# Complex state pairs in one tile: two-diagonal matrices, a scan over 64 cells and sums by three routes in a gated SSM and linear-attention kernel

## The chip, the cores and the metric

The kernel runs on one core of one Trainium2 chip. The metric is the device time of one execution in microseconds, as a median over runs. TensorE (PE) multiplies matrices into PSUM, VectorE (DVE) and ScalarE (ACT) compute between PSUM and SBUF, GpSimd (POOL) and SyncE (SP) here mostly issue DMAs.

## The reference

The input x has 2048 rows of 512 features. Two branches are mixed row by row with a gate g = sigmoid(x · gate_w):

```
Lam_bar = exp(dt * Lam)                      # 512 complex states
B_bar   = ((Lam_bar - 1) / Lam)[:, None] * B
h_t     = Lam_bar * h_{t-1} + B_bar x_t      # t = 0 .. 2047
a       = 2 * Re(C h_t) + x * Dskip
q, k, v = x @ wqkv                           # 32 heads of 16
pq, pk  = q @ w_phi, k @ w_phi               # per head
phi     = [softmax(p), softmax(-p)]          # 32 features for q and for k
b       = (phi_q (phi_k^T v)) / (phi_q sum(phi_k) + 1e-6) @ wo     # not causal
out     = g * a + (1 - g) * b
```

B, C, Lam and h are complex; re and im come as separate inputs, and all inputs are bf16. The output is bf16.

## The kernel before

**Tiling.** The 2048 rows are taken as 256 cells of 8 consecutive rows; a row's place in its cell is its residue r. `xT` holds x transposed with the rows sorted by residue, so that a strided slice gives all 256 cells of two residues r and r+4: 512 columns. Rows leave in 16 output tiles of 128 (128 cells of one residue), in the order of residues 7, 3, 5, 1, 0, 4, 2, 6. The 512 states are four tiles of 128 (index j), each with a re and an im half of its own.

**An order written by hand.** Every part of the work is a generator whose name is a token (`st_q` is `q0` to `q15`, and so on). The list `ORDER` of 841 tokens runs each generator on to its next `yield`, and no scheduler stands behind it: the list alone sets the order of instructions on every engine, and of the DMA issues on SP and POOL. `@n` after a token names the PSUM banks (eight in all) for the tiles it opens; `:D` puts an eviction or a scaling (`evac` L129, `scaled` L436 on ACT, L438 on DVE) on DVE where it would be on ACT.

```
    for tok in ORDER.split():
        tok, _, banks = tok.partition("@")
        tok, _, eng = tok.partition(":")
        sel["eng"] = "dve" if eng == "D" else "act"
        sel["banks"] = [int(b) for b in banks]
        next(st[tok])
```

**The attention branch.** `W`, `T`, `f`, `w` prepare weights and the first two tiles of x; x comes through SP in transposes (`Lx`), B in `Lb`, Q's weight in `Lq`, C in `Lc`. `k`, `v`, `q` (L483) make keys, values and queries for 128 rows by four matmuls each of 480 or 512 columns with an eviction (`Xq`, `vx`; `vx` is one of eight buffers). The features are two softmaxes over 16 values per head, for four tiles at a time: maximum tree `x`/`X` (L531), minimum `n`/`N`, subtractions into `EE` (L542, L548), exponential `e`/`E` (L554), sum tree and logarithm `s`/`S` (L562), division (L569 for keys; for queries only the ratio of the two sums is multiplied in, L581). For queries, `S` ends with two DMA transposes on SP into `phT` (`phT0` for the first four tiles, then two buffers in turn). `a` (L599) multiplies keys' features with values into two PSUM banks over all 16 tiles; in its loop L603 adds the gate's x · gate_w with matmuls of one column, 64 in all. `Y` masks the result into `KVm`. `o` (L835) multiplies `phT` with `KVm`, takes the logarithm of the denominator (L839), its negative exponential with the gate (L842), and scales into `on` (L848).

**The state branch.** With λ = Lam_bar, `M` and `M2` compute powers of λ in small tables, `D` makes nine sets of diagonal matrices `dg` (re, im and minus im of λ, λ², λ⁴) for the four j. `b` (L613) multiplies `BT` with two residues of x, `g` (L625) with the residues 1 and 5, 3 and 7, and adds in PSUM what the diagonals make of earlier rows of the cell: four real products for each complex one, over the two tiles re and im. In `g`'s second half, V (four rows summed, evicted by L129 into `vv`) is multiplied by λ⁴ (256 columns) and added, so that `vv` holds the sum over a cell. `i` makes rotation tables `T2c` and `T2s` for 256 cells, `z` turns the complex recurrence into real ones: two multiplications and two additions, a scan along 256 cells for re and one for im (L678), two multiplications (L681, L684) and two additions back, for each j. This gives the state at each cell's last row, in `H3`. `H` (`st_h4`) gives the state at row 3 of each cell from it (λ⁴ by two scalings and three additions on DVE). `h` then adds λ² times these to the local sums in `H1` (residues 1 and 5), and `p` adds λ times to those in `eb` (residues 0, 4 and 2, 6): each by row scalings on ACT or DVE, followed for j = 2 and 3 by three DVE operations, and for j = 0 and 1 by adding DMAs on POOL's queue (L648), which add one SBUF tile into another. `c` scales C by B_bar's factor into `C2`, again with an adding DMA for each j.

**The end.** `y` (L816) multiplies the states with `C2` for an output tile, eight matmuls of 512 columns; the skip term x · Dskip is added by four matmuls of 128 columns with a diagonal `Dd` (L823), or, for the tiles in the list `XD`, on DVE (`u`, L854). `O` transposes `on` to `oT` by DMA on SP (L862), `t` multiplies it with `Wo` into the same PSUM bank (L875) and evicts with the gate (L879 on DVE, L881 on ACT), `R` (L891) sends pairs of tiles out. `Z` (L316) is a matmul on a zero tile while the first inputs are under way. `G` (L748 and its neighbours) makes the sigmoid from the 16 gate columns.

Of the kernel before, what the change touches and what calls it, by code (L numbers as in the profile page):

```python
# [10 lines left out]
ALU = mybir.AluOpType  # L11
# [9 lines left out]
P = 128  # L21
# [15 lines left out]
N0 e4 z1 z1 H1 s2 g200 g200 g201 H1 g210@6 g211@3 g210 s4 H1 c1 g211 g210 q7@4 v4 s4 h0 h0 H1 H1 g210 h0 a2 a2 a2 a2
h1 h1 s4 s3 q4 s3 s4 g211 g211 q5@2 q5 q6@0 g211 X0 N0 q7 q6 g211 g210 X1 b300@7 g210 z2 b300 z2 p00:D z2 z2 z2 b311@4
p00 z2 b301@0 E0 X1 z2 b301 z2 E0 X1 v13@7 g301@6 s4 q9@0 b310@3 z2 b311 s4 z2 g301 g300@2 H2 S0 X1 S0 g301 g300 H2:D
S0 h1 b310 g310@4 g300 N1 S0 p10 c3 S0 h1:D h1 N1 s4 g311@6 q9 g311 g311 g311 g310 g310 g310 S0 S0 s4 p10 p10 H2 q10@2  # L40
g311 S0 g311 g310 g310 z3 z3 v13 H2 p00 H2 z3 z3 z3 v8@0 v8 v10@3 h0 z3 v10 p10 N1 v12@4 v12 z3 z3 S0 S0 h0 q8@0 p10
q8 z3 z3 v9@7 v9 v14@3 h2 h2:D H3:D H3:D p00:D v14 v15@0 v15 h2 v11@4 H3 a3 N1 a3 v11 a3 a3 a4 H3 q11@4 H3 a4 a4 h2 h2
a4 X1 N1 Y Y p11 h3 p11 y1@0 G y1 h3 y1 h3 Y Y q11 q10 X2 N2 G h3 h3 END q12@2 o1@4 o0@6 E1 X2 E1 o0 q14@1 q14 N2 o1
y6@3 y6 X2 N2 X2 S1 o0 o0 S1 q12 o1 y6 S0 p01 o1 q15@1 S1 N2 q15 q13@2 q13 p11 o3@6 y0@1 o3 S1 S1 p00 y0 X2 p30 o2@4
S1 o2 S1 o2 y0 N2 S1 o2 N3 o3 G Ld Ld E2 E2 y7@2 y7 S1 y7 y3@4 y3 y3 N3 p20 p01 X3 G o3 S2 O0 t0 t0 t1 t1 y5@5 S1 S1
X3 o4@6 O1 S2 o4 o4 N3 R0 o5@0 S2 S2 o5 o5 o4 o5 O2 S2 S2 N3 X3 X3 p30 y5 y5 y4@6 y4 S2 S2 o6@0 p01 p11 p01 o6 o6 X3
y2@7 p20 N3 E3 E3 p20 o6 p20 p20 t3 y2 y2 t2 t5 y4 t2 t3:D t4 t4 S2 S2 y10@4 o9@0 o9 o8@6 p30 p30:D p30 p11 y10 u9 S3
t5 o8 o8 o9 o8 o9 y11@5 o7@6 p01 y11 y9@0 S2 p21 S3 o7 S3 S3 O4 o7 o7 p31 p21:D y9 S3 S3 y8@1 S3 o10@6 R1 u8 o10 o10
S3 S3 y8 o10 p31 t8 o11@6 O3 t9 S3 S3 t6 o11 o11 p21 p31 t8 t9 y12@1 t7 p31:D y14@0 t6 t7 o11 o12@6 o12 p21 O5 p21
o13@2 u11 p31 y14 o12 o12 o13 y12 o13 R2 o14@6 o13 O6 o14 o14 o14 R4 u10 O7 y13@2 y13 o15@6 o15 o15 o15 t10 t10 R3 t11  # L50
t13 t11 u12 O8 u13 t12 t12 t13 u14 R5 t14 t14 R6 y15@54 y15 y15 t15 t15:D t15 R7 t15 R8 R8
# [4 lines left out]
XD = (8, 9, 10, 11, 12, 13, 14)  # L56
KO = tuple(range(16))
XLOADS = ((2, 2), (4, 2), (6, 2), (8, 2), (10, 2), (12, 2), (14, 2))
# [12 lines left out]
def kernel(  # L71
# [24 lines left out]
    PT = Pst // P  # L96
    NTI = S // P
# [42 lines left out]
    vec_n = const.tile([12, P], BF16, name="vec_n")  # L140
# [5 lines left out]
    C2 = const.tile([P, 2, PT, D], BF16, name="C2")  # L146
    warm = const.tile([P, D], BF16, name="warm")
    nc.vector.memset(warm[:], 0.0)
    nc.scalar.dma_start(out=Wc[:], in_=B_w_phi.rearrange("(k hl) e f -> (hl e) k f", hl=8))
    wk_nat, xn = C2[:, 0], C2[:, 1]  # L150
# [4 lines left out]
    for n, src in enumerate((A_Lambda_im, A_Lambda_re, A_log_dt)):  # L155
        nc.gpsimd.dma_start(out=vec_n[4 * n:4 * n + 4, :], in_=src.rearrange("(j p) -> j p", p=P))
# [6 lines left out]
    vec = const.tile([P, 5, KT], F32, name="vec")  # L163
# [791 lines left out]
```

## Time and profile before

| | |
|---|---|
| median of three runs | 151.08 us (150.99 to 151.36) |
| span of the profiled execution | 149.4 us |
| outside the span, against the median | 1.7 us |
| TensorE busy, matmuls | 142.8 us (96%), 1010 |
| VectorE busy, instructions | 139.0 us (93%), 338 |
| ScalarE busy, instructions | 125.1 us (84%), 222 |
| GpSimd busy, instructions | 26.6 us (18%), 42 |
| moved by DMA | 20.14 MB, mean 135 GB/s |

The span is the profiled execution's own time, from its first to its last instruction; the median is that of separate runs, which hold what lies before and after it. Times in the profile count from the span's start. An instruction's busy time runs from its start to its end, and neighbours on one engine may overlap a little, so the sum of the busy times is over the time that the engine needs in a full queue. In the rows, an operation is written as line, engine, operation, output<-input and shape (partitions x elements); "idle before" is the time that the engine stood before it, with what ended most of it.

### The profile page before, as it was taken

What the parts mean: (1) busy time and instruction counts of PE and PEld (TensorE: products, weight loads), DVE (VectorE), ACT (ScalarE), POOL (GpSimd) and SP (SyncE); (2) the same over time, 40 slices, a digit from 0 to 9 for tenths busy, and PEclk for the clock granted to TensorE, in tenths of its full rate; (3) what the DMA queues carried; (4) which work ended last, traced back from release to release, by engine and by line L of the source; (5) the groups of instructions that cost most, each with busy time, mean ns of one, the idle gap of its engine ahead of it and who ended that gap; (6) DMA issues with size and microseconds to landing.
All of it is one profiled execution on the core that took longest, in us unless ns stands there. A gap on an engine that the chain in (4) does not pass through costs nothing.

```text
span 149.4 us, 2839 instructions
## 1 busy us (share of the span) xinstructions
PE 142.8 (96%) x1010; PEld 73.8 (49%) x1010; DVE 139.0 (93%) x338; ACT 125.1 (84%) x222; POOL 26.6 (18%) x42
## 2 busy tenths in 40 slices
PE   6999999999999999999999999999999999999980
PEld 2844444545545444464444467555444554455450
DVE  2899999999999999999999999999999999986880
ACT  3479999999999999999999999999989996552000
POOL 7403700000000341022605236011004200000000
PEclk9999999999999999999999999999999999999999
DMA  4999999991220174008274999908999996998742
GB/s 118 222 235 174 142 202 176 246 189 33 54 91 0 26 114 77 0 0 140 38 107 70 166 175 183 210 7 133 103 238 218 184 186 77 227 207 197 209 148 71
DMA packets 52959, 20.14 MB, mean 135 GB/s; under 512 B 44496, under 2 KB 52432, under 8 KB 52944
## 3 DMA queue, kind: packets, MB, share of 16 engines
q1 hardware_dynamic: 48000, 15.44, 53.1%
q0 software_dynamic: 4000, 4.20, 18.6%
q10 hardware_dynamic: 944, 0.31, 0.8%
q8 instruction: 8, 0.13, 0.4%
q14 instruction: 7, 0.06, 0.1%
HBM read 2.91 MB, written 2.10 MB: 33 GB/s over the span
## 4 chain that ended last, share of the span: by engine, by line
ACT 67%; PE 24%; issue 3%; DVE 2%
ACT EE L554 15%; PE PS L816 11%; ACT Xq L129 9%; PE PS L875 7%; ACT CT L436 6%; ACT vx L129 5%; ACT dg L436 4%; ACT H L129 3%; ACT vv L129 3%; ACT eb L129 3%; ACT Bn L129 3%; PE PS L316 2%; PE PS L835 2%; ACT lg L562 2%; ACT m L436 1%
## 5 line engine op out<-in xcount | busy, mean ns | idle before, releaser
L554 ACT ACTIVATE EE<-EE 128x2048 bf16<-128x2048 bf16 x16 | 32.5, 2066 | 0.2 <-DVE EE L548 0.2
L483 PE MATMUL PS<-WKV,xT 128*128 128x480 bf16 (+1 forms) x128 | 29.3, 373 | 0.2 <-DMA xT<-in_A_x_dram 0.2
L483 PEld LDWEIGHTS <-xT 128*128 128x128 bf16 x192 | 18.1, 98 | 19.4 <-DMA xT<-in_A_x_dram 0.7
L129 ACT CAST Xq<-PS 128x480 bf16<-128x480 f32 x32 | 20.1, 735 | 0.5 <-PE PS L483 0.5
L625 PE MATMUL PS<-xT,BT 128*128 128x512 bf16 x64 | 15.9, 379 | 0.0
L816 PE MATMUL PS<-C,H 128*128 128x512 bf16 x64 | 15.4, 378 | 0.5 <-DVE on L848 0.2
L875 PE MATMUL PS<-Wo,oT 128*128 128x512 bf16 (+2 forms) x68 | 15.5, 367 | 0.0
L613 PE MATMUL PS<-xT,BT 128*128 128x512 bf16 x64 | 15.4, 379 | 0.0
L483 PE MATMUL PS<-Wq,xT 128*128 128x480 bf16 x64 | 15.1, 366 | 0.0
L848 DVE TENSOR_TENSOR on<-PS,rd 128x512 bf16<-128x512 f32 x16 | 10.7, 681 | 2.3 <-ACT rd L842 2.3
L881 ACT ACTIVATE ot<-PS,G 128x512 bf16<-128x512 f32 (+1 forms) x8 | 4.9, 639 | 9.1 <-PE PS L875 9.1
L436 ACT ACTIVATE CT<-H,dgs 128x1024 bf16<-128x1024 bf16 x9 | 12.1, 1349 | 0.0
L129 ACT CAST vx<-PS 128x512 bf16<-128x512 f32 x16 | 11.7, 793 | 0.0
L648 POOL DMA_DIRECT2D C<-CT x4 | 5.4, 1352 | 35.0 <-ACT rc L566 31.8
L531 DVE TENSOR_TENSOR sm<-EE 128x2048 bf16<-128x2048 bf16 (+1 forms) x9 | 10.0, 1108 | 0.1
L542 DVE TENSOR_TENSOR EE<-Xq,mx 128x2048 bf16<-128x2048 bf16 (+1 forms) x9 | 10.0, 1109 | 0.0
L548 DVE TENSOR_TENSOR EE<-mn,Xq 128x2048 bf16<-128x2048 bf16 (+1 forms) x9 | 10.0, 1107 | 0.0
L613 PEld LDWEIGHTS <-BT 128*128 128x128 bf16 x64 | 6.3, 98 | 7.2 <-issue 0.2
L569 DVE TENSOR_TENSOR EE<-EE,rc 128x2048 bf16<-128x2048 bf16 x8 | 9.8, 1234 | 0.0
L625 PEld LDWEIGHTS <-BT 128*128 128x128 bf16 x64 | 6.1, 98 | 7.0
L875 PEld LDWEIGHTS <-oT 128*128 128x128 bf16 x68 | 6.1, 98 | 6.5 <-DMA oT<-on 0.5
L531 DVE TENSOR_TENSOR sm<-sm 128x512 bf16<-128x512 bf16 (+2 forms) x18 | 9.3, 516 | 0.0
(185 smaller groups left out, 325.8 us busy)
## 6 DMA issues: line engine op xcount, KB each, us to landing
out_dram<-ot SPq DMA_DIRECT2D x7, 256.0 KB, 2.4
C<-CT POOLq DMA_DIRECT2D x4, 256.0 KB, 3.9
eb<-CT POOLq DMA_DIRECT2D x4, 256.0 KB, 4.9
eb<-dg POOLq DMA_DIRECT2D x4, 256.0 KB, 5.9
WKV<-in_A_x_dram SPq DMA_DIRECT2D x3, 256.0 KB, 3.1
WKV<-in_B_wqkv_dram SPq DMA_DIRECT2D x1, 512.0 KB, 5.6
Wo<-in_B_wo_dram SPq DMA_DIRECT2D x1, 512.0 KB, 4.8
H<-CT POOLq DMA_DIRECT2D x2, 256.0 KB, 3.3
```

What stands on the lines that cost most here:

```text
L129: nc.scalar.copy(out=out_ap, in_=in_ap)
L436: nc.scalar.mul(out=out_ap, in_=in_ap, mul=s_)
L483: MM(out=pt[:], lhsT=xT[:, kt, ti * P:(ti + 1) * P], rhs=W[:, kt, :], start=(kt == 0), stop=(kt == KT - 1))
L531: VT(out=dst, in0=cur[:, :, :, 0:n, :], in1=cur[:, :, :, n:2 * n, :], op=op)
L542: VT(out=half(EE, 0), in0=X5, in1=live["mx", p].to_broadcast([P, L, 8, Dh, 4]), op=ALU.subtract)
L548: VT(out=half(live["EE", p], 1), in0=live["mn", p].to_broadcast([P, L, 8, Dh, 4]), in1=X5, op=ALU.subtract)
L554: aexp(out=EE[:, l_:l_ + 2], in_=EE[:, l_:l_ + 2], func=ACT.Exp)
L613: MM(out=pb[:], lhsT=BT[:, ri, kt, j * P:(j + 1) * P], rhs=cells(kt, 2 * pr), start=(kt == 0), stop=(kt == KT - 1))
L625: MM(out=pgq[:], lhsT=BT[:, ri, kt, js], rhs=cells(kt, r1), start=(kt == 0), stop=False)
L816: MM(out=py[:], lhsT=hs[j][ri], rhs=C2[:, 1 - ri, j, c:c + w], start=(j == 0 and ri == 0), stop=False)
L848: VT(out=live["on", g_][:, u], in0=pn[:, :, :, 0:Dh], in1=rd[:].unsqueeze(3).to_broadcast([P, 2, 16, Dh]), op=ALU.mult)
L875: MM(out=py[:], lhsT=oT[:, g, :], rhs=Wo[:, g, c:c + w], start=False, stop=(g == HG - 1))
```

## The change

The 512 states become eight tiles (index m) of 64 states each, with the re parts in partitions 0 to 63 and the im parts of the same states in 64 to 127. Multiplying by a complex λ^k is then one product with a 128 by 128 matrix that has the re parts on its main diagonal and ± the im parts on two half diagonals (`dg[:, k, m]`, five powers: λ, λ², λ⁴, λ⁸, λ¹⁶). `LS` holds the sums of residues 0, 1, 2 (and 4, 5, 6), `HH` those of 7 and 3.

`g` goes two steps further: with λ⁸ and λ¹⁶ it sums pairs and then fours of cells (128 and 64 columns), evicts each into its place in `HH`, and `V2` takes the sums of four cells. The tables and the scan `z` run over 64 cells, four tiles m at a time (256 elements, `decay` with a zero at each tile's first cell); for the other half of the complex value a matmul with the matrix `Sw` swaps the partition halves. From the state of every fourth cell `sa` gives every second (λ¹⁶), `sb` each (λ⁸), `H` the middle of each cell (λ⁴): a product each, and an addition from PSUM into `HH` on DVE.

The list `UNITS` names how the last sums are made, by tile m: λ² into residues 1 and 5 by adding DMAs for m = 0 to 3 (`hd0`, `hd1`, two tiles each; four adding DMAs in all) and by row scalings with two DVE additions for m = 4 to 7 (`hk4` to `hk7`); λ into residues 0 and 4 by row scalings for all eight (`ek`); λ into residues 2 and 6 by a product and an addition from PSUM for all eight (`dp`). For the row scalings, `XX` copies `HH` with its partition halves swapped to `HHs`, four SP copies for each half of the tiles.

B is loaded to `C2` in two SP loads and transposed from there in four, instead of four transposes from DRAM. C is scaled into `CS`, added on DVE, and copied to `C2` by four SP copies (`C`). The gate's weight is a 481st column of Q's weight, `q` evicts it into `nge`, and `G` runs once for each group of four tiles. `XD` has four tiles instead of seven, `vx` seven buffers instead of eight, `phT` uses `phT0` and one more in turn. The list `ORDER` is written anew. Cut to its core:

```diff
-XD = (8, 9, 10, 11, 12, 13, 14)
+XD = (8, 9, 10, 11)
...
+ZB = 2
...
+        nc.gpsimd.dma_start(out=vec_n[MT * n:MT * n + MT, :].rearrange("m (d s) -> m d s", d=2),
+                            in_=src.rearrange("(m s) -> m s", s=HS).unsqueeze(1).to_broadcast([MT, 2, HS]))
...
-    Wq2 = const.tile([P, KT, DF], BF16, name="Wq2")
+    Wq2 = const.tile([P, KT, DF + 4], BF16, name="Wq2")
...
-    NVX = 8
+    NVX = 7
...
+    HHs = CS[:].rearrange("p r j d -> p (r j) d")
...
     def st_Lb():
         for ri, src in enumerate((A_B_re, A_B_im)):
-            for h in range(2):
-                trans(out=BT[:, ri, 2 * h:2 * h + 2, :], in_=src[:, 2 * h * P:2 * (h + 1) * P])
-                yield
+            nc.sync.dma_start(out=C2[ri * HS:(ri + 1) * HS], in_=src.rearrange("(m s) d -> s m d", s=HS))
+            yield
...
+        for m in range(0, MT, 2):
+            trans(out=BT[:, m:m + 2].rearrange("p m k c -> p (m k) c"), in_=C2[:, m:m + 2].rearrange("p m d -> p (m d)"))
+            yield
...
+    def st_D(k0, k1):
+        TT, TC = VT, nc.vector.tensor_copy
+        nk = k1 - k0
+        TC(out=dgv[0:HS, k0:k1].rearrange("p k m h f -> p k h m f"), in_=dgs[0:HS, k0:k1].unsqueeze(4).to_broadcast([HS, nk, 2, MT, 4]))
+        for h in range(2):
+            TC(out=dgv[HS:P, k0:k1, :, h, :], in_=dgs[HS:P, k0:k1, 1 - h].unsqueeze(3).to_broadcast([HS, nk, MT, 4]))
+        yield
+        for k in range(k0, k1):
+            TT(out=dg[:, k].rearrange("p m (h c f) -> p m h c f", h=2, f=4),
+               in0=I2[:].rearrange("p (h c f) -> p h c f", h=2, f=4).unsqueeze(1).to_broadcast([P, MT, 2, 16, 4]),
+               in1=dgv[:, k].unsqueeze(3).to_broadcast([P, MT, 2, 16, 4]), op=ALU.mult)
             yield
...
     def st_q(n):
-        pq = bank([P, DF], F32, "pq")
+        pq = bank([P, DF + 1], F32, "pq")
         tile_mm(pq, order[n], Wq2)
         yield
-        evac(xrel(n), pq[:].rearrange("p (hh x) -> p hh x", hh=8))
+        evac(xrel(n), pq[:, 0:DF].rearrange("p (hh x) -> p hh x", hh=8))
+        yield
+        VS(out=nge[:, n:n + 1], in0=pq[:, DF:DF + 1], scalar1=-Z_MAX, scalar2=-1.0, op0=ALU.max, op1=ALU.mult)
...
-            for kt in range(KT):
-                MM(out=live["acc"][1][:, 4 * KVW + ti:4 * KVW + ti + 1], lhsT=xT[:, kt, ti * P:(ti + 1) * P],
-                   rhs=gw_b[:, kt:kt + 1], start=False, stop=(n_ == NTI - 1 and kt == KT - 1), skip_group_check=True)
...
-        da, db = ((DG_LR, DG_NLI), (DG_LI, DG_LR))[ri]
-        MM(out=pgq[:], lhsT=dg[:, da, j, :], rhs=eb[j][:, 0, dst], start=False, stop=False)
-        MM(out=pgq[:], lhsT=dg[:, db, j, :], rhs=eb[j][:, 1, dst], start=False, stop=(dst == 0))
...
+    def st_g(m, dst):
+        pg = bank([P, N2], F32, "pg")
+        bx(pg, m, (1, 3)[dst])
+        yield
+        MM(out=pg[:], lhsT=dg[:, 0, m, :], rhs=LS[:, m, 2 * dst], start=False, stop=(dst == 0), skip_group_check=True)
         yield
         if dst == 0:
-            evac(U1[:, ri, :], pgq[:])
+            evac(LS[:, m, 1], pg[:])
             yield
             return
-        da, db = ((DG_MR, DG_NMI), (DG_MI, DG_MR))[ri]
-        MM(out=pgq[:], lhsT=dg[:, da, j, :], rhs=U1[:, 0, :], start=False, stop=False)
-        MM(out=pgq[:], lhsT=dg[:, db, j, :], rhs=U1[:, 1, :], start=False, stop=True)
-        yield
-        evac(V[:, ri, 0:NC], pgq[:, 0:NC])
-        yield
-        MM(out=pgq[:, NC:N2], lhsT=dg[:, da + 3, j, :], rhs=V[:, 0, 0:NC], start=False, stop=False, skip_group_check=True)
-        MM(out=pgq[:, NC:N2], lhsT=dg[:, db + 3, j, :], rhs=V[:, 1, 0:NC], start=False, stop=True, skip_group_check=True)
-        yield
-        evac(V[:, ri, NC:N2], pgq[:, NC:N2])
+        MM(out=pg[:], lhsT=dg[:, 1, m, :], rhs=LS[:, m, 1], start=False, stop=False, skip_group_check=True)
+        yield
+        evac(hc(m, 0, 1, NC, 1), pg[:, 0:NC])
+        yield
+        MM(out=pg[:, NC:N2], lhsT=dg[:, 2, m, :], rhs=hc(m, 0, 1, NC, 1), start=False, stop=False, skip_group_check=True)
+        yield
+        evac(hc(m, 0, 2, NC // 2), pg[:, NC:N2:2])
+        yield
+        MM(out=pg[:, NC + 1:N2:2], lhsT=dg[:, 3, m, :], rhs=hc(m, 0, 2, NC // 2), start=False, stop=False, skip_group_check=True)
+        yield
+        evac(hc(m, 1, 4, NC // 4), pg[:, NC + 1:N2:4])
+        yield
+        MM(out=pg[:, NC + 3:N2:4], lhsT=dg[:, 4, m, :], rhs=hc(m, 1, 4, NC // 4), start=False, stop=True, skip_group_check=True)
+        yield
+        evac(V2[:, m], pg[:, NC + 3:N2:4])
...
     def st_c(j):
-        scaled(C2[:, 1, j], CT[:, j, 0], dgs[:, S_BR, j:j + 1])
-        yield
-        scaled(C2[:, 0, j], CT[:, j, 1], dgs[:, S_NBR, j:j + 1])
-        yield
-        scaled(CT[:, j], CT[:, j], dgs[:, S_NBI, j:j + 1])
-        yield
-        add_by_dma(C2[:, :, j], CT[:, j])
-        yield
-
-    def st_z(j):
+        scaled(CS[:, 1, j], CT[:, 0, j], csp[:, 1, j:j + 1])
+        yield
+        scaled(CS[:, 0, j], CT[:, 1, j], csp[:, 2, j:j + 1])
+        yield
+        scaled(CT[:, :, j], CT[:, :, j], csp[:, 0, j:j + 1])
+        yield
+        VT(out=CS[:, :, j], in0=CS[:, :, j], in1=CT[:, :, j], op=ALU.add)
+        yield
+
+    def st_C():
+        for q, pq_ in ((0, 0), (1, 1), (0, 1), (1, 0)):
+            nc.sync.dma_start(out=C2[q * HS:(q + 1) * HS, pq_::2], in_=CS[pq_ * HS:(pq_ + 1) * HS, 1 - q])
...
+        v_ = V2[:, m0:m1].rearrange("p m c -> p (m c)")
+        pv = bank([P, w_], F32, "pz_")
+        MM(out=pv[:], lhsT=Sw[:], rhs=v_, start=True, stop=True)
+        yield
+        mc = sw.tile([P, w_], BF16, name="mc")
+        VT(out=mc[:], in0=v_, in1=tc_, op=ALU.mult)
+        yield
+        ms = sw.tile([P, w_], BF16, name="ms")
+        VT(out=ms[:], in0=pv[:], in1=ts_, op=ALU.mult)
+        yield
+        VT(out=mc[:], in0=mc[:], in1=ms[:], op=ALU.add)
+        yield
+        w = sw.tile([P, w_], BF16, name="w")
+        nc.vector.tensor_tensor_scan(out=w[:], data0=decay[:, m0:m1].rearrange("p m c -> p (m c)"), data1=mc[:], initial=0.0, op0=ALU.mult, op1=ALU.add)
+        yield
+        pw = bank([P, w_], F32, "pz_")
+        MM(out=pw[:], lhsT=Sw[:], rhs=w[:], start=True, stop=True)
+        yield
+        mc = sw.tile([P, w_], BF16, name="mc")
+        VT(out=mc[:], in0=w[:], in1=tc_, op=ALU.mult)
+        yield
+        ms = sw.tile([P, w_], BF16, name="ms")
+        VT(out=ms[:], in0=pw[:], in1=ts_, op=ALU.mult)
+        yield
+        VT(out=HH[:, m0:m1, ZP + 3:ZP + NC:4], in0=mc[:].rearrange("p (m c) -> p m c", m=n), in1=ms[:].rearrange("p (m c) -> p m c", m=n), op=ALU.subtract)
...
+    def st_s1(b):
+        n = MT // ZB
+        m0, m1 = b * n, (b + 1) * n
+        pd = bank([P, n, NC // 4], F32, "pd")
+        for m in range(m0, m1):
+            MM(out=pd[:, m - m0], lhsT=dg[:, 4, m, :], rhs=hc(m, -1, 4, NC // 4), start=(m == m0), stop=True, skip_group_check=True)
+        yield
+        addto(HH[:, m0:m1, ZP + 1:ZP + NC:4], pd[:])
...
+    def st_X(b):
+        n = MT // ZB
+        ms = slice(b * n, b * n + n)
+        for q in range(2):
+            for h in range(2):
+                nc.sync.dma_start(out=HHs[h * HS:(h + 1) * HS, ms, q * NC:(q + 1) * NC],
+                                  in_=HH[(1 - h) * HS:(2 - h) * HS, ms, ZP - 1 + q * (NC + 1):ZP - 1 + q * (NC + 1) + NC])
...
+    def by_dma(i, u, k):
+        plain = prevs if u < 2 else (lambda m: pair(LS[:, m, 1]))
+        for part, (src, sc_) in enumerate(((plain, dgs[:, k, 0, :]), (lambda m: pair(HHs[:, m]), nsn[:, k, :]))):
+            t = slot(2 * (i % 2) + part)
+            for e in range(2):
+                m = 2 * i + e
+                scaled(pair(t[:, e]), src(m), sc_[:, m:m + 1])
+                yield
+            add_by_dma(LS[:, 2 * i:2 * i + 2, u], t)
+            yield
+
+    def by_row(m, u, k):
+        plain = prevs if u < 2 else (lambda m: pair(LS[:, m, 1]))
+        t = slot(m % 4)
+        scaled(pair(t[:, 0]), plain(m), dgs[:, k, 0, m:m + 1])
+        yield
+        scaled(pair(t[:, 1]), pair(HHs[:, m]), nsn[:, k, m:m + 1])
+        yield
+        VT(out=t[:, 0], in0=t[:, 0], in1=LS[:, m, u], op=ALU.add)
+        yield
+        VT(out=LS[:, m, u], in0=t[:, 0], in1=t[:, 1], op=ALU.add)
+        yield
+
+    def by_pe(m, u, k):
+        pd = bank([P, N2], F32, "pd")
+        MM(out=pd[:], lhsT=dg[:, k, m, :], rhs=prevs(m) if u < 2 else LS[:, m, 1], start=True, stop=True)
+        yield
+        addto(LS[:, m, u], pd[:])
...
-        if r % 2:
-            src = H3 if r % 4 == 3 else H1
-            off = {7: ZP, 3: ZP + NC, 1: 0, 5: NC}[r] + a * P
-            hs = [[src[:, j, ri, off:off + P] for ri in range(2)] for j in range(PT)]
+        if r in (3, 7):
+            hs = [HH[:, m, ZP + (NC if r == 3 else 0) + a * P:][:, 0:P] for m in range(MT)]
         else:
             off = r // 4 * NC + a * P
-            hs = [[eb[j][:, ri, r % 4 // 2, off:off + P] for ri in range(2)] for j in range(PT)]
-        for j in range(PT):
-            for ri in range(2):
-                for py, (c, w) in zip(pys, halves):
-                    MM(out=py[:], lhsT=hs[j][ri], rhs=C2[:, 1 - ri, j, c:c + w], start=(j == 0 and ri == 0), stop=False)
-            if j % 2:
+            hs = [LS[:, m, r % 4, off:off + P] for m in range(MT)]
+        for m in range(MT):
+            for py, (c, w) in zip(pys, halves):
+                MM(out=py[:], lhsT=hs[m], rhs=C2[:, m, c:c + w], start=(m == 0), stop=False)
```

More of the change, by code (lines that the diff above doesn't have):

```diff
@@ L424, in st_D @@
[L424 to L431 removed]
+        for k in range(1, 3):
+            square(dgs[:, k], dgs[:, k - 1], outer, VT)
+            yield
@@ L841, in st_o @@
         rd = op_.tile([P, 2, 16], F32, name="rd")
[L842 removed]
+        aexp(out=rd[:], in_=ld[:], func=ACT.Exp, scale=-1.0, bias=nge[:, n:n + 1])
         yield
```

415 lines of the change are left out of this document (185 added, 230 removed).

## The prediction

> **What bounds the kernel now.** I read the page's busy times and slices first, then the ten-microsecond windows, the chain that ended last, and the timeline for the steps.
>
> ```profile
> PE 142.8 (96%) x1010; PEld 73.8 (49%) x1010; DVE 139.0 (93%) x338; ACT 125.1 (84%) x222; POOL 26.6 (18%) x42
> PE   6999999999999999999999999999999999999980
> DVE  2899999999999999999999999999999999986880
> ACT  3479999999999999999999999999989996552000
> ...
> 20.00:30.00 10.00, 10.00 (x52) 4.77 (x51) 10.00 (x23) 9.99 (x17) 0.00 (x0) 1.00 1.08 210
> 60.00:70.00 10.00, 9.94 (x91) 5.42 (x89) 10.00 (x18) 10.00 (x18) 1.73 (x2) 1.00 0.21 36
> 130.00:140.00 10.00, 10.00 (x74) 5.07 (x75) 7.68 (x15) 3.34 (x10) 0.00 (x0) 1.00 0.98 206
> ...
> ACT 67%; PE 24%; issue 3%; DVE 2%
> ```
>
> Three engines are full at once (the windows give PE, its weight loads, DVE, ACT, POOL, then the granted clock, 1.00, the share of the DMA engines and GB/s). ACT has room from 95 us on, DVE from 130 us, PE only at the end. The chain names ACT for the first 104 us and PE after that, but DVE is as full. So a change pays only where it lightens all three; the lightest relief counts, and a new wait on any of them is lost time.
>
> Busy times overlap within an engine, so I count steps: the time from one start to the next in a full queue. The chain has them for ACT and PE (start, time, engine, tile, line), the timeline for DVE.
>
> ```profile
> 47.58 0.47 ACT H L129
> 54.19 1.05 ACT CT L436
> 55.24 0.26 ACT vv L129
> 66.14 0.62 ACT phT L436
> 106.95 0.22 PE PS L823 x4
> 133.56 0.51 PE PS L835 x16
> 138.03 4.32 PE PS L875 x20
> 144.32 0.76 PE PS L875 x4
> ...
> 65.13 0.24 PE L603 MATMUL PS<-gw_b,xT 128*128 128x1 bf16 x4
> 65.23 0.41 PE L599 MATMUL PS<-vx,EE 128*128 128x68 bf16 x8
> ...
> 35.94 0.36 DVE L438 TENSOR_SCALAR C<-CT,dgs 128x512 bf16<-128x512 bf16 x1
> 36.20 0.70 DVE L531 TENSOR_TENSOR sm<-sm 128x1024 bf16<-128x1024 bf16 x1
> 36.80 0.96 DVE L429 TENSOR_TENSOR dg<-ident,dgv 128x1536 bf16<-128x1536 bf16 x1
> ...
> 58.28 0.31 DVE L673 TENSOR_TENSOR mc<-mc,ms 128x256 bf16<-128x256 bf16 x1
> 58.49 1.29 DVE L678 TENSOR_TENSOR_SCAN w<-ssm_par,mc 128x256 bf16<-128x256 f32 x2
> 59.67 0.29 DVE L531 TENSOR_TENSOR mn<-mn 128x256 bf16<-128x256 bf16 x1
> 59.85 0.45 DVE L681 TENSOR_TENSOR mc<-w,T2c 128x512 bf16<-128x512 bf16 x1
> 60.19 0.45 DVE L684 TENSOR_TENSOR ms<-w,T2s 128x512 bf16<-128x512 bf16 x1
> ...
> 104.32 0.69 DVE L848 TENSOR_TENSOR on<-PS,rd 128x512 bf16<-128x512 f32 x1
> 104.92 0.69 DVE L531 TENSOR_TENSOR mn<-Xq 128x1024 bf16<-128x1024 bf16 x1
> 105.52 0.17 DVE L748 TENSOR_SCALAR G<-G 128x16 f32<-128x16 f32 x1
> 105.60 0.69 DVE L581 TENSOR_TENSOR EE<-EE,rho 128x1024 bf16<-128x1024 bf16 x1
> ```
>
> PE: 512 columns 0.216 (4.32/20), 128 columns 0.055 (0.22/4), 68 columns 0.032 (0.51/16), one column 0.025 (65.13 to 65.23 for four); 256 columns are taken at 0.108, half of 512. DVE, bf16 in SBUF: 256 elements 0.20 (58.28 to 58.49), 512 0.34, 1024 0.60, a scaling of 512 0.26, a scan of 256 0.59 (1.18 for two), 512 out of PSUM 0.60, a tiny operation 0.08. ACT: eviction of 512 0.47, of 256 0.26; scaling of 512 0.62, of 1024 1.05.
>
> Counted over the program, the 1010 matmuls need 137.5 us of steps and the last ends at 145.1 (144.32 + 0.76). The first matmul on BT runs at 21.9 us with 17.2 us of steps ahead of it:
>
> ```profile
> L613 PE MATMUL PS<-xT,BT x64: 376/379/379, 21.9 to 74.8; 128*128 128x512 bf16 x64
> ```
>
> So 4.7 us go at the start and 2.9 us (145.1 − 137.5 − 4.7) are waits later; 4.3 us follow to the end of the span.
>
> **TensorE.** Gone: half of the matmuls that apply λ (16 of 32 of 512 columns) and λ² (8 of 16), 5.2; half of the λ⁴ ones (8 of 256), 0.9; the gate's 64 one-column matmuls, which the change puts into a 481st column of Q, 64 × 0.025 = 1.6. Added: eight 512-column products for the last sums, 1.7; λ⁴ again for the sums (8 of 256) and four swaps of 256, 1.3; 16 of 128 and 16 of 64 columns (at 0.032), 1.4; twelve diagonal products, since three fewer tiles take the skip term on DVE, 0.7. Net −2.6 by this, and −2.5 over the whole list: 978 matmuls, 135.0 us.
>
> The Trainium skill, "TensorE: Matmul & The Clock Gate", section "Back-to-back issue gap", gives streams 131 ns for 512 columns and 81 for 128. The rows say 216 and 55, so the measurement decides; by the page PE would have room everywhere, the sixteen added products of 128 columns would cost 0.4 us more than at 55 ns, and the time would be that of the third rival below.
>
> **VectorE.** Gone: the old scans, 4 × (four of 512, four of 256, two scans) = 13.4; the H stage, 4 × (0.34 + 0.40) = 3.0; the sums of j = 2, 3, 6 × (0.60 + 0.68) = 7.7; row scalings, 2.4; three skip tiles, two operations each of 0.66 (743 ns less the 0.09 that 0.69 overlaps into 0.60), 4.0; rotation tables, 3.4; nine diagonals, 2.7; an output scaling, 0.5. That is 37.1.
>
> ```profile
> L854 DVE SCALAR_TENSOR_TENSOR xd<-WKV,G,Drow 128x512 f32<-128x512 bf16 x7 | 5.1, 743 | 0.0
> ```
>
> Added: two 64-cell scans for all states, 2 × (four of 256 in SBUF, two of 256 from PSUM at 0.33, a scan) = 4.1; 14 additions of 512 from PSUM and two of 256, 9.1; 24 additions of 512 in SBUF, 8.2; C's additions, 4 × 0.60; tables 1.9; five matrices of 1024 and six small copies, 3.9; sixteen gate columns 1.3; the gate in four parts and small evictions 1.2. That is 32.1: net −5.0. The strided additions into HH have no row; between 0.33 and 0.60 for 256 moves the sum by under 1 us, and I take the PSUM rows.
>
> **ScalarE.** Fifteen scalings of 1024 and fourteen of 512 become 32 of 512: 24.4 to 19.8. Sixteen evictions of 256 become eight and some eighteen smaller, about 0.1 each. Three more outputs (0.57) come. Net −4.2, in an engine with room after 95 us: nothing for the end.
>
> **Queues.** POOL issues 4 adding DMAs for 14, off the path unless a sum waits. SP gets two loads of B, four copies of C, eight of HH, each held until its source is ready, with the output transposes queued behind. In the new order an oT transpose is followed by its first use after 3.5 to 6.8 us of matmul steps, in the old after 3.9 to 6.4.
>
> ```profile
> oT<-on SPq DMA_TRANSPOSE x9, 3.4
> phT<-EE SPq DMA_TRANSPOSE x8, 5.0
> eb<-CT POOLq DMA_DIRECT2D x4, 256.0 KB, 4.9
> L839 ACT ACTIVATE ld<-PS 128x32 f32<-128x32 f32 x16 | 3.9, 241 | 4.8 <-PE PS L835 4.6
> L835 PE MATMUL PS<-KVm,phT 128*128 128x68 bf16 x128 | 6.2, 194 | 0.3 <-ACT ot L881 0.3
> ```
>
> Three uses lie at 3.5 to 3.6 us, the median of landing; each may cost 0 to 1, I take 0.5 in all. The adding DMAs have 5 to 7 us before their readers against 4.9: nothing. Buffers shrink (vx from eight to seven, phT to two in turn), so a phT transpose waits until the group before last is read; its own first use follows after 6 us or more against 5.0: nothing, and 1 us for each us that it starts later.
>
> New handovers: the chain λ⁴, λ⁸, λ¹⁶, scan, then back down, passes PE → ACT or DVE → PE some 36 times more. A bare hop is 0.194 + 0.241 = 0.44 us, 15.8 us if none were covered, 0 if all are. The list interleaves states: four chains with `a`, `q`, `v` matmuls of 0.8 to 1.0 us between most hops, while around the second scan the order leaves nothing to spare (V2's eviction, swap, scan, swap). I take 1.0.
>
> **Sum.** PE −2.5; of its 2.9 us of waits, 1.0 goes since DVE, which it follows, gains more; new waits +1.5. The last matmul ends at 135.0 + 4.7 + 2.9 − 1.0 + 1.5 = 143.1, the span at 147.4. The median of the runs stands 1.7 above the profiled span (151.08 − 149.4), so 149.1 us. In the new order DVE's and PE's sums stay within 1.2 us of each other up to 130 us, so neither hides the other's stall.
>
> **Rivals.** *Handovers uncovered.* If a quarter of the 15.8 us stays bare, 4.0 instead of 1.0, the time is 152.1; above 3.0 bare it is slower. For: PE is in order and full, so a wait in one state's chain holds q and v behind it and DVE starves of new tiles. Against: the same kind of hop in the old stage (λ⁴ after V's eviction) costs little of the 2.9.
>
> *B comes late.* B is now loaded to SBUF, and SP waits for both loads before its first transpose.
>
> ```profile
> WKV<-in_B_wqkv_dram SPq DMA_DIRECT2D x1, 512.0 KB, 5.6
> BT<-in_A_B_re_dram SPq DMA_TRANSPOSE x2, 5.0
> 4.66 10.26 SPq L224 DMA_TRANSPOSE xT<-in_A_x_dram  x6
> ```
>
> Five xT at 1.7 end near 11.4, two loads of 0.57 are out at 12.6 and land between 18.2 and 22.6; BT's first pair lands 5.0 later, 23.2 to 27.6. The list has 21.4 us of steps ahead of its first use, so it is wanted at 26.1. The late end alone costs 1.5; with transposes from SBUF slower than from DRAM and four more queued behind, 3.1 at the second wait, on Q's weight: 152.2. It is slower once BT lands after about 28. For: DMA was full there (1.08 in the window 20 to 30). Against: the middle of my two ends is early.
>
> *VectorE's gain in full.* If PE's later waits shrink to 0.5, all 5.0 of DVE count: 149.4 − 5.0 + 1.7 = 146.1. For: DVE stood at 10.00 of 10 where PE waited. Against: PE runs at its steps there.
>
> **Chances.** 0.60 for the forecast (147.3 to 150.6), 0.16 for uncovered handovers, 0.12 for late B, 0.12 for the full gain. A measurement of this kernel tells 0.3%, 0.45 us, from no change: faster is 0.12 + 0.55 = 0.67, the tail of the forecast and the mild ends of the two waits give 0.08 for the same, 0.25 is slower. The range runs from 146.1 to 152.6.
>
> **What would show it.** Right: 978 matmuls in about 4.7 us of start plus 138 us; DVE near 134 us busy, ACT under 122; first use of BT near 26 us without a DMA wait; HH evictions and additions with waits of 0.1 to 0.4 each, 1 to 2 us in all. Wrong: a gap of PE and DVE between 24 and 36 us (B); PE slices of 8 or less between 70 and 95 us with waits on HH or LS (handovers); PE waiting for oT by more than 1 us in the last 40 us.

## The result, and the profile after

The changed kernel takes 158.69 us (median; 158.47 to 158.87) against 151.07 us (150.99 to 151.36) of the kernel before on the same chip: ratio 1.049, interval 1.047 to 1.051. It is 5% slower. The prediction was 149.1 us, at most 152.6. The times of lists 1 and 2 below leave out three runs (one and two of four) that were over 1.5% above the fastest of their kernel.

The page of the changed kernel: busy times, three slice rows, the chain by engine.

```profile
span 156.8 us, 2801 instructions
PE 144.2 (92%) x962; PEld 75.2 (48%) x978; DVE 139.2 (89%) x337; ACT 123.4 (79%) x236; POOL 21.0 (13%) x47
PE   6699998599999999989999999999989999999990
DVE  2669999999999999799999999999999999998810
PEclk9999999869999999999999999999999999999999
DVE 37%; PE 31%; ACT 19%; DMA 6%; issue 3%; ACTq 0%; DVEq 0%
```

The program has 978 matmuls, as forecast (the weight loads show all of them; 16 matmul records are missing). But the chain is now spread over three engines, no longer on one: each is waiting for another, in turn. DVE is as busy as before (139.0), though 5 us of its work went.

To see where the time went I take, for each matmul, its start less the sum of the steps of all matmuls ahead of it (the prediction's steps: 0.216 us for 512 columns and so on). This "lag" stays flat while PE runs at its steps and rises by each wait. Read at six points of the summed steps, with three kernels from the experiments below:

| lag, us, after so many us of steps | 5 | 25 | 50 | 80 | 100 | end | span |
|---|---|---|---|---|---|---|---|
| before (137.5 us of steps) | 4.2 | 4.7 | 4.9 | 5.4 | 6.3 | 7.5 | 149.4 |
| changed (135.0) | 6.5 | 11.0 | 11.3 | 14.5 | 16.1 | 17.6 | 156.8 |
| changed work, all three edits (below) | 4.6 | 6.0 | 9.2 | 12.4 | 14.1 | 15.5 | 154.7 |
| changed work, list 3 (below) | 9.6 | 9.7 | 9.8 | 10.6 | 14.4 | 14.8 | 154.0 |
| changed work, list 5 (below) | 4.3 | 4.5 | 5.8 | 7.8 | 8.9 | 10.5 | 149.8 |

PE's steps fell by 2.5 us, as forecast; its waits rose by 10.1. Of these, 6.3 are there after 25 us of steps. Three places make some 5.5 of them.

*The start, 1.8 us more.* PE's timeline of before and of the changed kernel (start, time, engine, line, operation, shape, idle before).

```profile
3.79 0.42 PE L299 MATMUL PS<-ident,C 128*128 128x128 bf16 x2
```

```profile
5.32 1.46 PE L319 MATMUL PS<-ident,CS 128*128 128x128 bf16 x12 [1.33 <-DMA CS<-in_B_wqkv_dram]
```

The new list begins with the half of the weight that ACT loads in one DMA of 256 KB, which lands at 5.3 us; the old one with a part that SP loads in 128 KB and that lands at 3.0. The size of this loss is that of one profile: two kernels below that begin with the same tokens (the logarithm, the interleaving) have a lag of 5.7 and 7.9 us after 5 us of steps, against 6.5 here.

*A stall of 2.2 us at 26.9.* The timeline of the changed kernel, all engines:

```profile
27.34 0.70 POOL L436 COPY decay<-ssm_par 128x512 f32<-128x512 f32 x1
27.61 0.58 DVE L566 TENSOR_TENSOR smf<-sm 128x128 f32<-128x128 bf16 x1
28.22 0.31 ACT L597 ACTIVATE lg<-smf 128x128 f32<-128x128 f32 x1 [1.84 <-DVE smf L566]
28.44 0.57 ACT L135 CAST vx<-PS 128x512 bf16<-128x512 f32 x1
29.06 2.10 PE L516 MATMUL PS<-WKV,xT 128*128 128x480 bf16 x8 [2.19 <-ACT vx L135]
30.95 1.06 PE L648 MATMUL PS<-xT,BT 128*128 128x512 bf16 x2
```

PE's next key tile needs the bank that v4's eviction frees. That eviction stands in ACT's queue behind the logarithm, the logarithm waits 1.84 us for the end of DVE's sum tree, and DVE is late. The list puts the logarithm (`s0`) two tokens ahead of that eviction; PE and ACT lose 2 us each, while DVE works on. The last row is the first use of BT: no DMA wait.

*The clock, some 1.5 us.* The one-microsecond windows (granted clock third from the end):

```profile
29.00:30.00 1.00, 0.94 (x5) 0.48 (x5) 1.00 (x1) 1.00 (x4) 1.00 (x2) 1.00 1.09 163
30.00:31.00 1.00, 1.00 (x6) 0.39 (x4) 0.94 (x6) 1.00 (x3) 0.40 (x2) 0.69 1.28 252
31.00:32.00 1.00, 1.00 (x4) 0.40 (x3) 1.00 (x1) 0.67 (x2) 0.00 (x0) 0.50 1.21 218
33.00:34.00 1.00, 1.00 (x4) 0.39 (x3) 0.93 (x5) 1.00 (x1) 0.00 (x0) 0.60 0.89 148
34.00:35.00 1.00, 1.00 (x7) 0.44 (x5) 1.00 (x5) 0.79 (x3) 0.00 (x0) 1.00 1.04 219
```

Some 1.3 us after PE resumes (29.06) the granted clock is 0.50 for 3.4 us (0.69 and 0.60 are windows of which 0.62 and 0.80 us lie at 0.50): PE counts as fully busy, and does half of its work.

From there on the lag rises in many steps of 0.3 to 1.7 us, none of them large.

DVE's own queue, in the timeline from 55 us:

```profile
55.55 1.21 DVE L566 TENSOR_TENSOR sm<-EE 128x2048 bf16<-128x2048 bf16 x1
56.79 0.69 DVE L566 TENSOR_TENSOR sm<-sm 128x1024 bf16<-128x1024 bf16 x1
57.40 0.68 DVE L566 TENSOR_TENSOR mx<-Xq 128x1024 bf16<-128x1024 bf16 x1
58.12 0.43 DVE L566 TENSOR_TENSOR mx<-mx 128x512 bf16<-128x512 bf16 x1
58.47 0.42 DVE L566 TENSOR_TENSOR sm<-sm 128x512 bf16<-128x512 bf16 x1
```

The second row reads what the first writes: it starts 0.03 us after the first has ended (55.55 + 1.21). The third does not: it starts 0.08 before the second ends. The fourth reads the third and is 0.04 late again. Each such pair costs about 0.115 us. The trace of the changed kernel has 50 of them, that of before 13. The steps that the prediction read from before all came from pairs that overlap.

### The profile page after: what moved, and what is told of

The parts are those of the page before. It is cut to its first block, busy times and chain, and to the rows that moved or that the text cites. A ratio compares the mean times of both kernels' runs of the same rounds, so it can differ in the third digit from the quotient of the medians.

```text
span 156.8 us, 2801 instructions
## 1 busy us (share of the span) xinstructions
PE 144.2 (92%) x962; PEld 75.2 (48%) x978; DVE 139.2 (89%) x337; ACT 123.4 (79%) x236; POOL 21.0 (13%) x47
## 4 chain that ended last, share of the span: by engine, by line
DVE 37%; PE 31%; ACT 19%; DMA 6%; issue 3%; ACTq 0%; DVEq 0%
PE PS L860 7%; ACT EE L589 6%; PE PS L516 5%; PE PS L643 5%; ACT CT L465 5%; DVE sm L566 5%; PE PS L916 4%; DMA LS<-CT 4%; PE PS L648 4%; DVE mx L566 3%; DVE EE L577 3%; DVE EE L583 3%; DMA CS<-in_B_wqkv_dram 3%; DVE mn L566 2%; DVE LS L735 2%
## 5 line engine op out<-in xcount | busy, mean ns | idle before, releaser
L860 PE MATMUL PS<-C,LS 128*128 128x512 bf16 (+1 forms) x100 | 23.3, 362 | 1.1 <-ACT ot L922 0.6
L135 ACT CAST Xq<-PS 128x480 bf16<-128x480 f32 x31 | 16.9, 570 | 0.3
L516 PE MATMUL PS<-Wq,xT 128*128 128x481 bf16 x64 | 15.2, 366 | 0.9 <-DVE V L137 0.9
L916 PE MATMUL PS<-Wo,oT 128*128 128x512 bf16 (+2 forms) x66 | 15.5, 366 | 0.1
L135 ACT CAST LS<-PS 128x512 bf16<-128x512 f32 x24 | 14.0, 604 | 2.0 <-PE PS L648 1.7
L860 PEld LDWEIGHTS <-LS 128*128 128x128 bf16 x104 | 9.3, 97 | 10.6 <-issue 1.4
L684 POOL DMA_DIRECT2D LS<-CT x4 | 4.9, 1220 | 60.0 <-DMA CS<-HH 53.8
L465 ACT ACTIVATE CT<-HH,dgs 128x512 bf16<-128x512 bf16 x16 | 11.1, 715 | 1.3 <-DMA LS<-CT 1.0
L465 ACT ACTIVATE CT<-CS,nsn 128x512 bf16<-128x512 bf16 x16 | 11.3, 710 | 0.0
L922 ACT ACTIVATE ot<-PS,G 128x512 bf16<-128x512 f32 (+2 forms) x12 | 7.5, 639 | 4.2 <-PE PS L916 4.2
L648 PEld LDWEIGHTS <-BT 128*128 128x128 bf16 x64 | 6.6, 105 | 7.9 <-issue 2.3
```

Of the source, the lines that this page charges most:

```text
L135: nc.scalar.copy(out=out_ap, in_=in_ap)
L465: nc.scalar.mul(out=out_ap, in_=in_ap, mul=s_)
L516: MM(out=pt[:], lhsT=xT[:, kt, ti * P:(ti + 1) * P], rhs=W[:, kt, 0:pt.shape[-1]], start=(kt == 0), stop=(kt == KT - 1))
L648: MM(out=pb[:], lhsT=BT[:, m, kt, :], rhs=cells(kt, 2 * pr), start=(kt == 0), stop=(kt == KT - 1))
L860: MM(out=py[:], lhsT=hs[m], rhs=C2[:, m, c:c + w], start=(m == 0), stop=False)
L916: MM(out=py[:], lhsT=oT[:, g, :], rhs=Wo[:, g, c:c + w], start=False, stop=(g == HG - 1))
```

## The experiments

The theories go by letters: A, what is lost before 36 us is carried to the end since PE is full; B, DVE's queue is slower than its steps; C, the new chain of handovers costs PE its time between 70 and 100 us; D, the waits belong to the list that was handed in; E, they belong to the new work, in whatever order. Every kernel below has the changed kernel's instructions (the control: those of before) and differs only in `ORDER`. That includes the banks, and with the start of before two operations more that `:D` puts on DVE in place of ACT (DVE x339 and ACT x234 for 337 and 236).

**Three edits of the list, and all at once.** The start as in the kernel before; the logarithm behind v4's, k8's and k10's evictions; DVE's trees interleaved, so that fewer operations follow the one that they read (32 such places in the list for 60).

```diff
-Z@0 B B B Z Z Z Z Z W10@1 Lk Lk W00@2 W10 W00 W00 Lx W01@3 W01 T0@1 Lx W11@2 T1@4 V@5 ...
+Z@0 Lk Lk B:D B Z Z Z Z Z B B W01@1 Lx Z W00@2 Lx W00 W00 W01 W01:D Lx W11@3 W10@4 W11 ...
```
```diff
-... v5 s0 k11 s0 s1 Lb v4 x2 k12@5 Db k8 k10 n2 ...
+... v5 s0 k11 s1 Lb v4 x2 k12@5 Db k8 k10 s0 n2 ...
```
```diff
-... N3 N3 ek0 X3 X3 ...
+... N3 X3 ek0 N3 X3 ...
```

> The changed kernel with the first 50 tokens of the list in the order of the kernel before: the weight half that SyncE loads is transposed first, the 512 KB load of V's weight comes after two transposes of x. Theory A (the loss is made in the first 36 us, by a start 1.8 us later and a stall of 2.4 us that also halves the clock for 1.5 us, and a full TensorE carries it to the end): TensorE's first x products come 1.8 us earlier, 158.7 - 1.8 = 156.9. Theory B (VectorE sets the pace; its queue is slower than counted, since operations stand directly behind the one whose result they read): VectorE starts up to 2.9 us earlier as well, 155.8 to 156.9. Theory C (the new chain lambda^4 to lambda^16, scan and back costs the time between 70 and 100 us): 158.7, since that stage still waits for itself.

> The changed kernel with one token moved: the logarithm of the first keys' sums (s0's fifth step) comes on ScalarE behind the evictions of v4, k8 and k10 instead of ahead of them. VectorE's queue is as before. Theory A: the 2.4 us stall of TensorE at 27 us and the 1.5 us of low clock behind it go, 158.7 - 3.9 = 154.8. Theory B: TensorE gains its stall but VectorE, which is late by itself, does not: 158.2 to 158.7. Theory C: 158.7.

> The changed kernel with only VectorE's tokens of the trees (maximum, minimum, sum) put in turn with each other, so that 28 of the 60 operations that stand directly behind the one whose result they read no longer do. Each such pair cost 0.115 us more in the trace (34 ns bare and the lost overlap of 80 ns). Theory B: 28 x 0.115 = 3.2 us less VectorE time, 155.5 to 156.3. Theory A: at most 0.5 us, since TensorE's early stalls stay: 158.2 to 158.7. Theory C: 158.2 to 158.7.

> The three reorderings together. Theory A: 158.7 - 1.8 - 3.9 = 153.0, the third adds nothing. Theory B: 158.7 - 2.9 - 3.2 = 152.6, the second adds nothing. Both: near 151 or less, since each engine's loss would then be gone. Theory C: 158 or more.

Measured against 158.69 (ratio to before 1.049, 1.047 to 1.051): the start 158.38 us (1.044, 1.038 to 1.050), the logarithm 158.29 (1.045, 1.040 to 1.051), the interleaving 158.24 (1.041, 1.035 to 1.047), all three 156.35 (1.031, 1.027 to 1.035). The intervals of the single edits overlap that of the changed kernel, so none of them alone is clear of the noise; all three together are. Each edit does at its place what it should, and almost nothing to the end: with the start alone the lag at 5 us is 4.9 and at 25 us 10.2 again, since the stall grows to 2.35 us. With all three it is 6.0 at 25 us (5.0 less than the changed kernel) and 15.5 at the end (2.1 less). PE's and DVE's waits of that kernel (total, times, longest):

```profile
PE PS L648 <- ACT LS L135: 1.2, 2, 1.0
DVE nge L550 <- ACT Xq L135: 1.2, 1, 1.2
DVE CS L467 <- POOL csp L447: 1.2, 1, 1.2
PE PS L516 <- DVE V L137: 0.9, 1, 0.9
PE PS L516 <- DVE Xq L137: 0.7, 1, 0.7
PE PS L670 <- DVE dg L458: 0.7, 1, 0.7
```

New waits stand in every stage, on other operations. Theory A, as it was put, is wrong: time won early is not carried to the end either. So is B: with the interleaving DVE's busy time falls by 1.9 us, to 137.3, and the time by half a microsecond, not by the 2.4 to 3.2 forecast. C fits the single edits and fails for all three, where it said 158 or more. So the question became whether any order of this work does better.

**Two lists from a replay.** To find orders I replayed the list with the traces' step times and moved tokens; the replay is only where the lists come from, and their times are those of the chip. The first two left out that DMAs queue behind each other.

> The changed kernel, the same instructions on the same engines, with a new order list: tokens moved, where no token passes one whose data, bank or buffer it shares, so that fewer of them wait; found by replaying the step times of the traces through the four queues. Theory D (the waits belong to the list: each of three full engines waits in turn for another, so a cure in one place is taken back in the next, as the three reorderings together gave 2.3 us where the stalls that they took away were 5): TensorE's 17.6 us of start and waits fall to the 7.5 of the kernel before or near it, its steps are 135.0 against 137.5, so 149 to 152. Theory E (the waits belong to the work: products, evictions and additions of a new chain that stand one behind the other whatever the list): no order helps, 155 to 158.

> A second list found in the same way from another start, to tell the method from one lucky list. Theory D: 149 to 152, within 1 us of the first. Theory E: 155 to 158.

160.84 us (159.86 to 162.06; ratio 1.062, 1.055 to 1.070) and two runs of 160.19 and 161.99 us: worse than the list handed in, and outside what either theory forecast. The second shows a stall and the clock again:

```profile
PE PS L648 <- ACT LS L135: 2.8, 1, 2.8
PE PS L916 <- DMA oT<-on: 1.9, 1, 1.9
DVE nge L550 <- ACT Xq L135: 2.7, 3, 1.1
```

**Two lists with the DMA queue in the replay**, and with the clock and the wait of the gate column as the traces show them.

> The same instructions in a third list. [...] Theory D (the waits belong to the list): 149 to 152. Theory E (they belong to the work): 155 to 158.

> A fourth list, made like the third from another start. Theory D: 149 to 152. Theory E: 155 to 158.

155.14 us (ratio 1.025, 1.020 to 1.030) and 155.75 us (1.029, 1.025 to 1.032): both in E's range, none in D's. But list 3 is telling in the table: it loses 9.6 us at the start, where it waits for the weight and for log dt's load, then nothing at all up to 50 us, and 3.5 between 80 and 90 us, in the stage of the second scan and the sums behind it.

```profile
PE PS L319 <- DMA CS<-in_B_wqkv_dram: 2.9, 1, 2.9
PE PS L860 <- ACT CT L465: 1.2, 1, 1.2
PE PS L750 <- DVE HH L735: 0.8, 1, 0.8
PE PS L341 <- DMA vec_n<-in_A_log_dt_dram: 0.5, 1, 0.5
```

If D holds, the same body with the start of before is 4.7 us faster.

**Lists 5 and 6: the start of before, and a body made in the same way.**

```diff
 ORDER of list 5
+Z@0 Lk Lk B:D B Z Z Z Z Z B B W01@1 Lx Z W00@2 Lx W00 W00 W01 W01:D Lx W11@3 W10@4 W11 Z B f1@5
+f1 Lv f0@1 T1@0 W10:D f0:D T0@3 f2@2 V@6 T1 T0:D V f3@4 f2 k1@7 f3:D P P U P2 U k0@3 P2 P2 Lx
 ...
```

> Same instructions as the changed kernel in a fifth list: its first 38 tokens follow the kernel before's start (weights loaded on SP first, x's first transposes as early), the rest is made like list 3's. Theory D (the waits belong to the list that was handed in, not to the new work): list 3 took 155.1 us with its matmuls 9.6 us behind their steps at 5 us of steps, where the kernel before has 4.9; with this start 4.7 us of it come back: 150.5 us, 149 to 152, about the kernel before. Theory E (the waits belong to the new work: the chain of the eighth and sixteenth powers with a handover at each step, row sums that read each other's results): the 3.6 us that list 3 still lost between 80 and 90 us of steps stay, and new waits take the place of the start's, as in the run of all three edits (5.0 us early in hand, 2.1 us at the end): 153 to 155 us.

> A sixth list with the same start and another body. D: within 1 us of the fifth list and both under 152 us. E: both over 153 us. If the two differ by over 2 us, the body of the list alone decides more than the start does.

151.45 us (151.32 to 151.51; ratio 1.0034, 1.0020 to 1.0048) and 152.59 us (1.0118, 1.0101 to 1.0135). List 5 is where D said, list 6 misses D's 152 by 0.6 and stays under E's 153. The same instructions that took 158.69 us take 151.45 in another order: 7.2 of the 7.6 us lost go with the list. List 6 has the same start and is 1.1 us slower, so the body counts too, if less. The page of list 5, and then its longest waits on PE after the start:

```profile
span 149.8 us, 2811 instructions
PE 141.0 (94%) x978; PEld 73.5 (49%) x978; DVE 136.4 (91%) x339; ACT 121.8 (81%) x234; POOL 25.4 (17%) x47
PE   6899999999979999999999988999999999989990
DVE  2799999999999999999999999999999999969720
PE 51%; DVE 33%; DMA 7%; issue 3%; POOL 2%; ACT 1%; POOLq 0%; DVEq 0%
```

```profile
PE PS L516 <- DVE nge L550: 1.1, 1, 1.1
PE PS L878 <- DMA phT<-EE: 0.6, 1, 0.6
PE PS L742 <- DVE HH L731: 0.6, 1, 0.6
```

DVE's busy time falls to 136.4 (8 bare pairs left), ACT's to 121.8, and no stall of PE is over 1.2 us, so the clock holds. The lag grows by 6.2 us after the start, against 3.3 in the kernel before. These 2.9 us eat the 2.5 us of fewer steps. Two of the places are new work: 1.1 us for a bank whose gate column DVE evicts late, and 2.3 us from 75 to 85 us of steps, where the scan's results come down through `sa`, `sb` and `H`.

**A control, and a seventh list.** The list of the kernel before was rearranged in the same way; and list 5 once more, with the replay now set to the times of list 5's trace.

> Control: the kernel before with the same instructions, its first 38 tokens kept and the rest of its list rearranged by the same means that made the fifth list. If the new work is as good as the old one and the fifth list is just a better list than the one handed in, a rearranged list should also help the kernel before: the replay that found it puts it 1.7 us ahead of its own list, so 149.4 us, 148.9 to 150.5; then the changed work (151.45 in list 5) is some 1 to 2 us slower than the old at equal care for the list. If the kernel before's list has nothing left to gain, it stays at 151 or loses: 150.7 to 153; then the two kinds of work are equal within 1 us.

> The changed kernel's instructions in a seventh list: list 5 with small moves, in which GpSimd's work beside VectorE is weighed more and the waits behind the gate columns are shorter. Theory D (the waits belong to the list): list 5's 151.45 less the 0.7 that the replay gains: 150.7 us, 150.0 to 151.4, for the first time ahead of the kernel before. Theory E (the last 3 us of waits belong to the work): 151.2 to 152, no better than list 5.

Both expectations failed: 156.71 us (ratio 1.036, 1.034 to 1.039) for the old work, 157.28 us (1.038, 1.034 to 1.041) for the new. List 7 holds list 5's lag up to 70 us of steps (5.8 us for 6.0), loses 4.0 in small waits up to 85 (list 5: 2.7), and then, at one place, 2.7 us and the clock behind it. Its timeline, and its one-microsecond windows:

```profile
98.12 1.19 POOL L684 DMA_DIRECT2D LS<-CT  x1 [2.48 <-ACT rd L885]
99.70 1.19 POOL L684 DMA_DIRECT2D LS<-CT  x1 [0.38 <-issue]
103.31 0.72 ACT L465 ACTIVATE CT<-HH,dgs 128x512 bf16<-128x512 bf16 x1 [2.08 <-DMA LS<-CT]
103.33 0.10 PEld L811 LDWEIGHTS <-dg 128*128 128x128 bf16 x1 [2.81 <-DMA LS<-CT]
```

```profile
102.00:103.00 1.00, 0.00 (x0) 0.00 (x0) 1.00 (x3) 0.00 (x0) 0.00 (x0) 1.00 1.11 214
105.00:106.00 1.00, 1.00 (x4) 0.30 (x2) 1.00 (x4) 1.00 (x2) 0.00 (x0) 0.50 2.04 131
106.00:107.00 1.00, 1.00 (x4) 0.37 (x3) 0.86 (x4) 1.00 (x1) 0.00 (x0) 0.50 0.91 43
```

The second adding DMA lands 3.6 us after its issue began (99.70 to 103.3), the list had left it less, and PE and ACT stand for it together. The kernel before's instructions lose 5.5 us in a worse order, the changed kernel had lost 7.6. So the control shows how much a list is worth for the old work too, and settles nothing about which work would win with the best list for each: the best seen, side by side, are 150.89 us for the old and 151.45 for the new.

One loss stayed in every list. Between 70 and 90 us of steps, where the second scan and the way back from it stand, the lag of all twelve kernels with the new work grows by 2.5 to 6.3 us (the changed kernel 2.6, list 5 2.8), that of the kernel before by 0.4 and that of the control by 1.2. In list 5 this is 2.4 of the 2.9 us by which its lag grows more than before's. So 1 to 2 us look like a price of the new work (theory E, for this part), but what of it is the chain of handovers, and whether another order hides it, was not separated.

## Why the prediction was wrong

**TensorE's steps, −2.5 us: right.** 978 matmuls, 135.0 us of steps. In list 5 the last matmul ends at 145.7 us, in the kernel before at 145.3.

**"Then 4.7 us at the start": wrong by 1.8.** The prediction kept the start of before, though the new list had put another load first. The runs with the old start gave 4.3 to 4.9 at once.

**"Of its 2.9 us of waits, 1.0 goes ... new waits +1.5": the step that failed.** The lag at the end was to be 8.1 and is 17.6: 1.8 of the 9.5 from the start, 7.7 from waits, for which +0.5 stood in the sum. They were priced by the kernel before's waits, as if the new list would be as well fitted as the old one. The experiments say that this was the assumption that carried the result: with the work unchanged, lists gave 151.45 to 161.1 us (list 2, the mean of its two runs).

**VectorE, −5.0: right in steps, wrong in what it brings.** The steps, by the same prices, sum to 131.5 for 136.4. The busy time was to be 134 and is 139.2: 37 more bare pairs cost 4.3 us (3.0 of it busy time), two operations stretched beside GpSimd's cost 0.6, and the other 1.6 us were not traced. So nothing of the gain is left. That pairs differ was to be read in before's trace, which has 13. With all but 8 of the pairs gone, list 5 has 136.4, half of the forecast gain. The relief of "1.0 since DVE gains more" was therefore not there, and with it the third rival, the full gain.

**ScalarE under 122: nearly.** 123.4, and 121.8 in list 5.

**B comes late: place right, cause wrong.** The prediction named a gap of PE and DVE between 24 and 36 us as B's sign. PE's gap is there (DVE has none), but BT's first pair landed at 21.7 us, ahead of the 23.2 to 27.6 forecast, and is used at 30.95 us without a wait for a DMA; the bank behind the logarithm made the gap. Transposes from SBUF were not slower: BT's four took 2.7 to 4.4 us to land, against the 5.0 read from before.

**Handovers: 1.0 forecast, mis-sized in every list.** In list 5, 2.3 us at the second scan; in list 3, 3.5; over the whole stage at least 2.5 in each of twelve lists. The first two lie between the forecast and the rival "uncovered" (4.0); alone, 2.3 to 3.5 in place of 1.0 would have given 150.4 to 151.6. Whether a better order hides it was not shown.

**oT 0.5, adding DMAs nothing: half right.** The waits of the changed kernel:

```profile
PEld L916 <- DMA oT<-on: 0.5, 1, 0.5
ACT CT L465 <- DMA LS<-CT: 1.0, 1, 1.0
```

List 7 shows what an adding DMA costs when its cover is gone: 2.7 us and the clock.

The chance of 0.25 for slower was too small because every rival was one mechanism of the work. None of them was "the list itself": many waits of 0.3 to 2 us, each on another operation, with three engines full and nothing to take them up.

## What to carry to other kernels

Where several engines are over 90% busy and the order is written by hand, a sum of steps is a floor and not a forecast: an order made anew cost the same instructions anything from 0.6 to 9.7 us over the kernel before, and the well-fitted order of the old kernel is worth 5.5 us against the one other order tried. Before a change with a new list is judged, fit the list, more than once (of seven lists made here two came within 1.2% of the kernel before): keep the proven start, let no engine's queue hold an eviction behind a late result, put a foreign operation between a DVE operation and its reader, give each DMA a margin over its median landing. Where curing one wait gives nothing, cure several together: here no single edit was clear of the noise, three gave 2.3 us together, and a whole new order 7.2. And a wait that stays in every order tried, as the one in the stage of the second scan, is best priced as the new work's own.

## What the runs showed of the hardware

**The clock falls to half for a window of 3.41 us after a window in which PE stood for over 2 us.** After gaps of 2.19 (changed kernel), 2.35 (start alone), 2.69 (list 7) and 2.79 us (list 2) the granted clock was 0.50 for 3.41 us each time: up to 1.7 us more on top of the gap. It began between 0.15 us before the end of the gap and 1.3 us behind it. The windows do not start with the gap: in each of these traces the low stretch and the fall after the last matmul begin a whole number of 3.413 us apart (in the changed kernel 30.38 and 156.67 us, 37 windows). In the window just ahead of the low one PE stood for 2.09, 2.14, 2.27 and 2.63 us. After gaps of 1.86 (list 2), 2.02 (list 1) and 2.07 us (the control) the clock did not fall; they left at most 1.95 us of idle in one window, since two of them lay across an edge. The Trainium skill, "TensorE: Matmul & The Clock Gate", section "What's actually happening", gives a window of about 3.4 us, free-running, both for an idle PE before the clock is halved and for a busy one before it returns. The length of the window and its running free agree; the window ahead of the low clock was idle for only 2.09 to 2.63 us of it here, and the measurement decides.

**Reading the result of the operation just ahead costs DVE about 0.115 us**: 0.034 of bare gap and 0.08 of overlap lost (rows from 55.55 above).

**GpSimd beside DVE stretched two DVE operations.** The sum to `smf` takes 0.58 us beside GpSimd's copy to `decay` (27.34 to 28.04, above) and half of that alone:

```profile
35.39 0.28 DVE L566 TENSOR_TENSOR smf<-sm 128x128 f32<-128x128 bf16 x1
```

The Trainium skill, "GPSIMD Engine Reference", section "8. Key points", says that GpSimd shares its SBUF interfaces with VectorE and contends with operations of two SBUF inputs; this row agrees, but it is the exception. Of 28 DVE operations of the changed kernel that ran beside GpSimd's and whose shape also ran alone, 26 took within 0.06 us of their usual time, most of them with two inputs; the other one that did not is a minimum at 25.12 us (0.33 us longer). Both ran beside a GpSimd operation of 512 columns (`decay`, `Dd`).

**A gate column waits for its neighbour.** DVE's eviction of column 481 stands until ScalarE has evicted the other 480 of the same bank (1.2 and 2.7 us in the waits above). Whether the bank or the program's own order makes that wait was not tried.
